# Seven products of halves in both GEMMs, on blocks of 896 tokens, in an attention and MoE kernel

## The chip, the cores and the metric

One Trainium2 chip; the kernel runs on one of its cores. The metric is the device time of one execution in microseconds, the median of several. TensorE is called PE, VectorE DVE, ScalarE ACT, GpSimd POOL and SyncE SP; almost all transfers are issued from SP's queue.

## The reference

```python
# attention, per batch b and head h (8 x 8, 576 tokens, 64 wide)
q_s = softmax(q, over the 64 columns)
k_s = softmax(k, over the 576 tokens)
kv  = k_s.T @ v                    # 64 x 64
out = q_s @ kv                     # 576 x 64
x = all heads side by side         # 4608 tokens x 512
# MoE
h = x @ w_in                       # 512 -> 2048
g = h * clip(h + 3, 0, 6) / 6
y = g @ w_out                      # 2048 -> 512, float32
```

The weights come as float64. Each float32 operand of the two GEMMs is held as a sum of two parts, hi + lo (type fp32r), and a product is made in three matmuls: hi·hi, hi·lo and lo·hi.

## The kernel before

The 4608 tokens go in nine blocks of 512 (`TB`). w_in and w_out are cut into sixteen pieces `f` of 128 columns (rows) of the hidden width; a pair is two neighbouring pieces.

**Blocks 0 and 1** are plain. For each f, `gemm1` (12 matmuls of 512 columns into the PSUM tile `ph`) makes 128 hidden features for 512 tokens; ACT (L560) and DVE (L561) make the gate g; `split` (L121: ACT casts the hi part at L123, an engine, mostly DVE, subtracts at L124) makes g_hi and g_lo; `gemm2` (12 matmuls of 512 columns) adds g times w_out into four accumulators `po`, tokens on partitions. During block 0, `load_w` and `decode` bring in the sixteen weight pieces and turn them into hi and lo parts; DVE does most of that. During block 1, `fast_weights` (L454 to L465) makes for each pair of w_in, on DVE, the four sums of quarters that seven-product multiplication (Strassen's method in Winograd's form) needs, splits them, and stores seven pieces of 256 KB per pair in DRAM (`wf`).

**Blocks 2 to 8** run pair by pair in `fast_pair`. GEMM1 of a pair is seven products; each is six matmuls of 256 columns (half of the 512 tokens), with its weight piece fetched back from DRAM into a ring of twelve (`fetch`, `RING`). Three PSUM tiles x, y, z (ring `ph`, two banks, and `pz`) gather the products; ACT and DVE (L517 to L543) add them up, gate and split. GEMM2 of the pair before stays plain: 24 matmuls of 512 columns. They are laid between the products by `fill(4)`, `fill(8)`, so that PE has work while ACT and DVE read a PSUM tile.

**Attention** for the next block runs as a generator, `attention`, advanced a step at a time from the block's loop. For a head pair `hp`: the softmax of q in a transposed layout (`q_softmax_t`, L284 to L302: five DVE passes over 512 columns and small copies `swap` on POOL), the softmax of k (L333, L348, L351), the matmuls `pkv`, and `px`, which is x for 128 features by 512 tokens, in hi and lo parts. `x_factors` makes from x the seven token-side operands: four differences on POOL (L437 to L440), splits on ACT and DVE.

**Order of the work.** From block 1 on, PE's matmuls keep the program's order (`keep_in_program_order`). The other engines' instructions are put in an order by a scheduler at build time, and run in that order.

Of the kernel before, what the change touches and what calls it, by code (L numbers as in the profile page):

```python
# [18 lines left out]
P = 128  # L19
TB = 512  # L20
QD = 32
NC4 = TB // P
EPS = 1e-9
# [7 lines left out]
def attention_moe(  # L31
# [8 lines left out]
    out: bass.AP,  # L40
):

# [20 lines left out]
    NT, DM = out.shape  # L63
    NB = NT // TB
    NFC = w.shape[0]
    NCC = DM // P
# [3 lines left out]
    SHIFT = S - TB  # L70

    const = ctx.enter_context(tc.tile_pool(name="const", bufs=1))
    wp = ctx.enter_context(tc.tile_pool(name="wp", bufs=1))
# [35 lines left out]


    def place(f, dt, name):
        return wp.tile([P, 4 * DM], dt, name=name, tag=f"w{f}")
# [8 lines left out]
    def split(hi, lo, src, engine=nc.vector):  # L121

        nc.scalar.copy(hi, src)  # L123
        engine.tensor_sub(lo, src, hi.bitcast(F32))  # L124

    def load_w(f, sides=(0, 1)):
        if f not in raws:
            raws[f] = place(f, U32, f"raw{f}")
        a, b = 2 * DM * sides[0], 2 * DM * (sides[-1] + 1)
        nc.sync.dma_start(  # L130
            raws[f][:, a:b], w[f].rearrange("p s n -> p (s n)")[:, a:b]
        )

    def decode(f):

# [15 lines left out]
        v = moe.tile([P, n], F32, name="v", bufs=2)  # L151
# [15 lines left out]
    FAST = 2  # L167
    x_tiles = {}

    def x_block(j):  # L170
        if j not in x_tiles:
            x_tiles[j] = (
                xp.tile([P, NCC, TB], F32R, name=f"x_hi{j}", tag="x_hi"),
                xp.tile([P, NCC, TB], F32R, name=f"x_lo{j}", tag="x_lo"),
            )
        return x_tiles[j]
# [24 lines left out]
    def kv_of(j, hp, ke, vt):  # L201

        pkv = ps_a.tile([P, TB], F32, name="pkv", tag="pa")
# [8 lines left out]
        kv = att.tile([P, P], F32, name="kv", bufs=5)  # L212
# [10 lines left out]
    def kv_split(j, hp):  # L223
        kv = kvs[j, hp]
        kvs[j, hp] = (
            att.tile([P, P], F32R, name=f"kv_hi{j}_{hp}", tag="kv_hi", bufs=5),
            att.tile([P, P], F32R, name=f"kv_lo{j}_{hp}", tag="kv_lo", bufs=5),
        )
        split(*kvs[j, hp], kv)

# [6 lines left out]

# [22 lines left out]
    def k_softmax(j, km, ke, kt):  # L260

# [3 lines left out]
        pool, tag = (ps_a, "pa") if j else (ps_o, "po")  # L265
        pe = pool.tile([P, TB], F32, name="pe", tag=tag)
        pe2 = pool.tile([P, TB], F32, name="pe2", tag=tag)
# [6 lines left out]
    NG = TB // QD  # L274
# [5 lines left out]

# [6 lines left out]
    def q_softmax_t(qt):  # L287

# [12 lines left out]
        qT = moe.tile([P, 2 * DM], F32, name="m", bufs=1)[:, 0:TB]  # L301
# [3 lines left out]
    def attention(j, hp):  # L305

        early = j < 2  # L310
        if not j:
            kt, qt, qT, vt, ke = first[hp]
        else:
            if j < B:
                kt = att.tile([P, S], F32, name="kt", bufs=1)
                nc.sync.dma_start(kt, kT[j, hp])
                ke = att.tile([P, NCH, P], F32, name="ke", bufs=2)
                if not early:
                    nc.sync.dma_start(ke, k[j, hp].rearrange("p c h d -> p c (h d)"))
                vt = att.tile([P, NCH, 2, D + 1], F32, name="vt", bufs=2)  # L320
                nc.sync.dma_start(vt, v[j, hp])
            qt = att.tile([P, TB], F32, name="qt", bufs=2)
            nc.sync.dma_start(qt, q[j, hp] if early else qf[j - 2, hp])
            if early:
                qt = qt.rearrange("p (c h d) -> p c h d", c=NC4, h=2)

        if j < B:
            km = att.tile([P, 1], F32, name="km", bufs=2)
            if early:
                ks = k_softmax(j, km, ke, kt)  # L330
# [35 lines left out]
        if j < B:  # L366
            kv_of(j, hp, ke, vt)
            if not early:
                kv_split(j, hp)
# [382 lines left out]
```

## Time and profile before

| | |
|---|---|
| time, median of 3 runs | 916.43 us (916.09 to 917.74) |
| span of the profiled execution | 914.7 us |
| median less span | 1.7 us |
| mean granted TensorE clock | 0.989 |
| first product of block 2 starts | 248.35 us |
| matmuls | 5380 |
| moved by DMA | 182.04 MB, mean 199 GB/s |

No time of its own is listed for the profiled execution; its span is the first to the last instruction, and the 1.7 us are what lies around it. A busy time of an engine is the part of the span in which at least one of its instructions ran; instructions of one engine overlap a little, so the sum of their durations is some per cent more. A matmul's duration in the groups (394 ns for 512 columns) is from its start to its modelled end and holds the pipeline; how long it keeps PE is read from the distance of starts.

### The profile page before, as it was taken

What the parts mean: (1) busy time and instruction counts of PE and PEld (TensorE: products, weight loads), DVE (VectorE), ACT (ScalarE), POOL (GpSimd) and SP (SyncE); (2) the same over time, 40 slices, a digit from 0 to 9 for tenths busy, and PEclk for the clock granted to TensorE, in tenths of its full rate; (3) what the DMA queues carried; (4) which work ended last, traced back from release to release, by engine and by line L of the source; (5) the groups of instructions that cost most, each with busy time, mean ns of one, the idle gap of its engine ahead of it and who ended that gap; (6) DMA issues with size and microseconds to landing.
All of it is one profiled execution on the core that took longest, in us unless ns stands there. A gap on an engine that the chain in (4) does not pass through costs nothing.

```text
span 914.7 us, 15285 instructions
## 1 busy us (share of the span) xinstructions
PE 863.9 (94%) x5380; PEld 740.6 (81%) x5380; DVE 629.0 (69%) x1265; ACT 456.1 (50%) x938; POOL 147.2 (16%) x330
## 2 busy tenths in 40 slices
PE   4799998999989999999999999999989999999998
PEld 3478766778878888888878888888878898999887
DVE  7999997888876666766666666767666655444333
ACT  6897653444444444445444444445544444444333
POOL 4112232121312120212011211112121201010000
PEclk8899999999999999999999999999999999999999
DMA  9973242538666667666676667765755565557641
GB/s 373 415 311 98 85 151 100 161 117 299 190 221 193 213 197 255 204 212 200 223 225 196 213 210 252 212 208 176 237 162 166 169 207 170 176 165 228 183 140 46
DMA packets 96842, 182.04 MB, mean 199 GB/s; under 512 B 9728, under 2 KB 24064, under 8 KB 94720
## 3 DMA queue, kind: packets, MB, share of 16 engines
q1 hardware_dynamic: 96192, 180.03, 60.9%
q10 hardware_dynamic: 576, 1.05, 0.3%
q8 instruction: 43, 0.70, 0.3%
q14 instruction: 31, 0.25, 0.1%
HBM read 156.93 MB, written 24.12 MB: 198 GB/s over the span
## 4 chain that ended last, share of the span: by engine, by line
PE 66%; DVE 10%; DMA 5%; ACT 2%; issue 1%; POOL 1%; SPq 0%; DVEq 0%; ACTq 0%; POOLq 0%
PE po L91 32%; PE ph L91 25%; PE pz L91 4%; DMA out_dram<-ob 3%; DMA qt<-in_qf_dram 2%; PE px L91 2%; PE pkv L91 2%; DVE m L302 1%; DVE x_lo L124 1%; DVE qT_lo L124 1%; DVE x_hi L124 1%; POOL swap L284 1%; ACT qT_hi L123 1%; DVE ob L591 1%; ACT v L433 1%
## 5 line engine op out<-in xcount | busy, mean ns | idle before, releaser
L91 PE MATMUL po<-w,w 128*128 128x512 f32 x1008 | 261.5, 394 | 2.2 <-DVE ob L591 2.2
L91 PEld LDWEIGHTS po<-w,w 128*128 128x128 f32 x1008 | 178.4, 189 | 32.8 <-DVE ob L591 4.0
L91 PE MATMUL ph<-w,w 128*128 128x256 f32 x1008 | 140.1, 284 | 16.7 <-DVE second L526 16.3
L91 PE MATMUL ph<-x_lo,w 128*128 128x256 f32 (+1 forms) x800 | 151.5, 304 | 2.1 <-ACT second L522 1.1
L91 PEld LDWEIGHTS ph<-w,w 128*128 128x128 f32 x1008 | 132.1, 190 | 24.2 <-DVE second L526 18.7
L91 PE MATMUL ph<-x_hi,w 128*128 128x256 f32 (+1 forms) x592 | 137.7, 337 | 3.1 <-DVE w L124 1.8
L91 PEld LDWEIGHTS ph<-x_lo,w 128*128 128x128 f32 x800 | 116.9, 189 | 16.2 <-ACT second L522 1.4
L91 PEld LDWEIGHTS ph<-x_hi,w 128*128 128x128 f32 x592 | 92.9, 191 | 16.7 <-DVE w L124 3.2
L123 ACT CAST w<-g 128x512 fp32r<-128x512 f32 x112 | 69.5, 620 | 73.7 <-DVE g L535 39.3
L124 DVE TENSOR_TENSOR w<-g,w 128x512 fp32r<-128x512 f32 x112 | 77.7, 694 | 27.5 <-ACT w L123 26.6
L91 PE MATMUL po<-w 128*128 128x512 f32 x336 | 86.2, 393 | 0.0
L124 DVE TENSOR_TENSOR qT_lo<-m,qT_hi 128x512 fp32r<-128x512 f32 x28 | 23.5, 839 | 80.8 <-ACT qT_hi L123 80.8
L91 PE MATMUL po<-w,g_hi 128*128 128x512 f32 x256 | 69.5, 409 | 2.2 <-ACT g_hi L123 2.0
L91 PEld LDWEIGHTS po<-w 128*128 128x128 f32 x336 | 59.6, 189 | 10.4 <-ACT w L123 0.5
L533 ACT ACTIVATE g<-ph,three 128x256 f32<-128x256 f32 x56 | 26.5, 472 | 72.2 <-PE ph L91 72.2
L284 POOL COPY swap<-qm 32x16 f32<-32x16 f32 x112 | 35.8, 319 | 159.2 <-DVE qm L292 133.4
L91 PEld LDWEIGHTS po<-w,g_hi 128*128 128x128 f32 x256 | 47.4, 191 | 14.4 <-ACT g_hi L123 4.0
L535 DVE SCALAR_TENSOR_TENSOR g<-g,ph 128x256 f32<-128x256 f32 x56 | 23.3, 415 | 45.2 <-ACT g L533 44.9
L526 DVE TENSOR_TENSOR second<-second,ph 128x256 f32<-128x256 f32 x56 | 22.8, 406 | 43.8 <-ACT second L525 43.7
L91 PE MATMUL pz<-x_hi,w 128*128 128x256 f32 x336 | 51.5, 290 | 0.0
L91 PEld LDWEIGHTS pz<-x_hi,w 128*128 128x128 f32 x336 | 46.5, 190 | 4.4
L525 ACT COPY second<-ph 128x256 f32<-128x256 f32 x56 | 20.9, 373 | 55.4 <-PE ph L91 55.3
(123 smaller groups left out, 1290.5 us busy)
## 6 DMA issues: line engine op xcount, KB each, us to landing
w<-wf SPq DMA_DIRECT2D x392, 256.0 KB, 2.9
raw<-in_w_dram SPq DMA_DIRECT2D x16, 1024.0 KB, 12.9
out_dram<-ob SPq DMA_DIRECT2D x36, 256.0 KB, 2.8
vt<-in_v_dram SPq DMA_DIRECT2D x28, 325.0 KB, 3.7
wf<-w SPq DMA_DIRECT2D x16, 512.0 KB, 4.6
kt<-in_kT_dram SPq DMA_DIRECT2D x28, 288.0 KB, 3.1
ke<-in_k_dram SPq DMA_DIRECT2D x24, 320.0 KB, 3.1
qt<-in_qf_dram SPq DMA_DIRECT2D x28, 256.0 KB, 3.0
```

Source lines behind the costliest of these rows:

```text
L91: nc.tensor.matmul(out, lhsT, rhs, start=start, stop=stop, skip_group_check=goes_on)
L123: nc.scalar.copy(hi, src)
L124: engine.tensor_sub(lo, src, hi.bitcast(F32))
L284: nc.gpsimd.tensor_copy(swap[r : r + QD], stat[o : o + QD])
L302: nc.vector.transpose(qT, qt)
L433: nc.scalar.copy(x[:, TB:], px)
L525: nc.scalar.copy(second[:, HT:], x)
L526: nc.vector.tensor_add(second[:, HT:], second[:, HT:], y)
L533: nc.scalar.activation(a, h, AF.Relu, bias=three, scale=1.0)
L535: nc.vector.scalar_tensor_tensor(a, a, 6.0, h, op0=ALU.min, op1=ALU.mult)
L591: nc.vector.tensor_scalar_mul(ob, po[t], 1.0 / 6.0)
```

## The change

- **Blocks.** Blocks 0 and 1 stay plain. The other 3584 tokens go in four large blocks of 896 (`SB`), halves of 448 (`TH`).
- **Phase 1** (`phase1`): GEMM1 of all eight pairs, 56 products of six matmuls of 448 columns; the seven products of neighbouring pairs are interleaved by a table (`AT`). PSUM tiles x1, y1, z1 come from a pool of six banks. g of the whole block stays on chip as float32 (`g_pairs`), not split.
- **Phase 2** (`phase2`): GEMM2 by the same seven products, again 56 of six matmuls of 448 columns, grouped by product (`ORDER2`, eight pairs each), with the output features on partitions. For each product `make` splits a quarter of g (or a running sum of quarters, L589, L591, L593) into a ring of four (`gf`), three products ahead of PE. The output is written transposed, and the host side of `kernel` turns it back.
- **Weights.** Both w_in and w_out are now kept as seven pieces per pair. `sum_weights` makes the sums: ACT copies the hi part of four quarters (L430), four DMAs issued from POOL add the lo part in flight (`accum_op=ALU.add`, L431), DVE makes four sums, `split` follows. Thirteen of the sixteen calls are in block 1, three (`late_sums`) in the first phase 1. The plain quarters are stored by `plain_weights`.
- **Attention** of a large block (`sb_attention`): q's softmax over 896 columns, one or two new batches of k and v per head pair, and `px` as float32 matmuls without hi and lo parts; x stays float32, and `factors` makes the seven operands on ACT and DVE, none on POOL.
- **Memory.** The weights lie in two pools that are closed in turn (`next_stage`): the operands and the ring of fetched pieces (five tiles of two pieces) take the place of w_0 to w_9, the tiles g0 to g6 that of w_10 to w_15.

The core of the diff:

```diff
+TH = 448
+SB = 2 * TH
...
-    ps_h = ctx.enter_context(tc.tile_pool(name="ps_h", bufs=2, space=PSUM))
-    ps_o = ctx.enter_context(tc.tile_pool(name="ps_o", bufs=4, space=PSUM))
+    ps = ctx.enter_context(tc.tile_pool(name="ps", bufs=6, space=PSUM))
...
+    def sb_attention(s, hp):
+        t0 = START + s * SB
+        need = [b for b in range(t0 // S, (t0 + SB - 1) // S + 1)]
...
+        qT = q_softmax_t(qt)
+        yield
...
+        for c in range(2):
+            px = bank_a("px")
...
+                    mm(px[:, lo:hi], kvs[b, hp], qT[:, sl], True, True)
+            nc.scalar.copy(x[:, hp, c * TH : (c + 1) * TH], px[:, 0:TH])
...
+    AT = {1: 0, 0: 1, 3: 3, 2: 4, 4: 6, 5: 9, 6: 12}
+    SLOTS1 = sorted((7 * p + AT[n], p, n) for p in range(NPAIR) for n in range(7))
+    SLOTS1 = [(p, n) for _, p, n in SLOTS1]
+    ORDER2 = (1, 2, 3, 0, 4, 6, 5)
+    SLOTS2 = [(p, n) for n in ORDER2 for p in range(NPAIR)]
...
+    def sum_weights(pair, side):
+
+        w4 = moe.tile([P, 2 * DM], F32, name="v", bufs=3)
...
+            for n, src in enumerate(halves(pair, side)):
+                t = w4[:, n * HT : (n + 1) * HT]
+                nc.scalar.copy(t, src[:, 0].bitcast(F32))
+                nc.gpsimd.dma_start(t, src[:, 1].bitcast(F32), accum_op=ALU.add)
...
+        nc.vector.tensor_add(s1, a21, a22)
+        nc.vector.tensor_sub(s2, s1, a11)
+        nc.vector.tensor_sub(s3, a11, a21)
+        nc.vector.tensor_sub(s4, a12, s2)
+        for i in range(2):
...
+            split(four[:, :, 0], four[:, :, 1], src)
+            for k_ in range(2):
+                block = (S1, S2, S3, S4)[2 * i + k_]
+                keep(pair, side, block, dst[:, k_ * TB : (k_ + 1) * TB].bitcast(F32))
...
+    def factors(s):
...
+        parts(X11, x11)
+        yield
+        parts(X21, x21)
+        yield
+        t = moe.tile([P, 2, TB], F32, name="r", tag="gp", bufs=3)[:, :, 0:TH]
+        nc.vector.tensor_sub(t, x22, x12)
+        parts(T3, t)
...
+    def phase1(s, between):
...
+            for c in range(2):
+                cs = slice(c * P, (c + 1) * P)
+                for m, (w_, f_) in enumerate(((w_hi, f_hi), (w_hi, f_lo), (w_lo, f_hi))):
+                    mm(to, w_[:, cs], f_[:, c], n in (0, 1, 2) and not c and not m, c == 1 and m == 2, True)
+            used(s, 0, i)
...
+                if n == 1:
+                    nc.scalar.copy(h11, x)
+                if n == 0:
+                    nc.vector.tensor_add(h11, h11, z)
+                    relu6(h11, temp()[:, 0, 0:TH], h11)
+                if n == 3:
+                    nc.scalar.copy(h21, x)
+                if n == 2:
+                    nc.scalar.copy(h22, y)
+                if n == 4:
+                    nc.vector.tensor_add(h22, h22, x)
+                if n == 5:
+                    relu6(h12, temp()[:, 0, 0:TH], x)
+                if n == 6:
+                    nc.vector.tensor_add(h21, h21, y)
+                    r = temp().rearrange("p a n -> p (a n)")[:, 0:SB]
+                    relu6(gb, r, gb)
+                    nc.vector.tensor_sub(h12, h22, h12)
...
+    def phase2(s, between):
...
+        def make():
...
+            t = ring[:, i % 4]
+            split(t[:, 0], t[:, 1], src)
+            ready[i] = t
+            if n == 1:
+                nc.vector.tensor_add(a, a, b)
+            if n == 2:
+                nc.vector.tensor_sub(b, d, a)
+            if n == 0:
+                nc.vector.tensor_sub(c, c, a)
...
-    for j in range(FAST, NB):
-        for pair in range(NFC // 2):
...
-            gs = fast_pair(j, pair, slot)
-            fill()
-            pend.append(work(j, [2 * pair, 2 * pair + 1], gs))
+    for s in range(NS):
...
+        def between1(i):
+            if not s and i in (12, 24, 36):
+                sum_weights(*late_sums[i // 12 - 1])
+            if i % 5 in (1, 3):
+                next(step, None)
+
+        def between2(i):
+            if i > 16 and i % 2:
+                next(step, None)
+            if i in (31, 33, 35, 37, 39, 41, 43):
+                next(fac, None)
+
+        phase1(s, between1)
+        phase2(s, between2)
```

Two places show how the instructions stand. On PE, before, in the middle of a fast block (`ph` and `pz` take products, `po` is GEMM2, `pm` and `pkv` attention; the names behind the arrow are the moving and the standing operand):

```order
L91 MATMUL ph<-x_hi_311,w_737 128x256 x6
L91 MATMUL po<-w_737,w_980 128x512 x4
L91 MATMUL ph<-w_335,w_737 128x256 x6
L91 MATMUL ph<-w_306,w_798 128x256 x6
L91 MATMUL po<-w_737,w_980 128x512 x8
L97 MATMUL pm<-ident,kb 128x128
L91 MATMUL ph<-x_lo_312,w_798 128x256 x6
L91 MATMUL po<-w_798,w_1039 128x512 x8
```

On PE now, the first products of a phase 1 (x, y, z are its PSUM tiles, `right` the token-side operands, `left` the fetched weight pieces):

```order
L87 MATMUL x_2537<-right_2444,left 128x448 x6
L87 MATMUL z_2546<-right_2447,left 128x448 x6
L87 MATMUL x_2537<-right_2492,left 128x448 x6
L87 MATMUL y_2601<-right_2452,left 128x448 x6
L87 MATMUL x_2537<-right_2495,left 128x448 x6
L87 MATMUL x_2622<-right_2444,left 128x448 x6
L87 MATMUL z_2633<-right_2447,left 128x448 x6
```

The four or eight matmuls of GEMM2 that stood between two products are gone; between two products into the same tile x stand products of the other tiles and of the neighbouring pair.

On DVE, before, about one pair of a fast block (`first`, `second` and `ph` belong to the products, `w` takes the split g, `x_hi`, `x_lo` the split operands, `kv`, `qT_lo` and `m` are attention):

```order
L519 TENSOR_TENSOR first<-first,pz 128x256
L124 TENSOR_TENSOR kv_lo_2_3732<-kv,kv_hi_2_3731 128x128
L535 SCALAR_TENSOR_TENSOR g<-g,first 128x256
L124 TENSOR_TENSOR qT_lo<-m,qT_hi 128x512
L124 TENSOR_TENSOR x_hi_311<-v,x_hi_311 128x256
L124 TENSOR_TENSOR x_lo_312<-v,x_lo_312 128x256
L302 STREAM_TRANSPOSE m<-qt 128x512
L526 TENSOR_TENSOR second<-second,ph 128x256
```

On DVE now, in the fourth group of products of the first phase 2 (`gf` is the ring of split quarters of g, `g` a tile of g, `right` and `x_1535` belong to the operands of the next block):

```order
L593 TENSOR_TENSOR g_2544<-g_2544 128x448
L124 TENSOR_TENSOR right_3792<-r,right_3792 128x896
L124 TENSOR_TENSOR gf<-g_2855,gf 128x448
L593 TENSOR_TENSOR g_2631<-g_2631 128x448
L647 TENSOR_TENSOR v<-v 128x448 x2
L509 TENSOR_TENSOR x_1535<-x_1535 128x2x448
L124 TENSOR_TENSOR gf<-g_2963,gf 128x448
L124 TENSOR_TENSOR right_3839<-x_1535,right_3839 128x896
L124 TENSOR_TENSOR gf<-g_3075,gf 128x448
```

Between two splits of g, one for each product of PE, now stand a subtraction of 448 columns and one or two operations of 896 columns.

More of the change, by code (lines that the diff above doesn't have):

```diff
@@ L201, in kv_of @@
     def kv_of(j, hp, ke, vt):
[L203 removed]
+        pkv = bank_a("pkv")
         for c in range(NCH):
@@ new lines, in attention_moe, with x_of @@
+    held = {}
+    def x_of(s):
+        if "x" not in held:
+            held["x"] = xp.tile([P, NCC, SB], F32, name="x32", tag="xa")
+        return held["x"]
+    def sb_attention(s, hp):
+        t0 = START + s * SB
+        need = [b for b in range(t0 // S, (t0 + SB - 1) // S + 1)]
+        qt = att.tile([P, SB], F32, name="qt", bufs=2)
+        nc.sync.dma_start(qt, qf[s, hp])
+        loads = {b: load_k(b, hp, tokens=True) for b in need if (b, hp) not in kvs}
+        new = {}
+        for b, (kt, ke, vt) in loads.items():
+            km = att.tile([P, 1], F32, name="km", bufs=2)
+            nc.vector.tensor_reduce(km, kt, axis=AX.X, op=ALU.max)
+            kb = att.tile([P, P], F32, name="kb", bufs=2)
+            nc.gpsimd.tensor_copy(kb, km.broadcast_to([P, P]))
+            new[b] = ke, vt, kb
+        qT = q_softmax_t(qt)
@@ new lines, in attention_moe, with keep, halves @@
+    SLOT = [{pn: i for i, pn in enumerate(slots)} for slots in (SLOTS1, SLOTS2)]
+    NSLOT = len(SLOTS1)
+    late_sums = [(7, 0), (6, 1), (7, 1)]
+    kept = [dr.tile([P, NSLOT, TB], F32, name=f"wf{i}") for i in range(2)]
+    spare = dr.tile([P, len(late_sums), TB], F32, name="spare")
+    def keep(pair, side, block, src):
+        to = kept[side][:, SLOT[side][pair, PRODUCT[block]]]
+        nc.sync.dma_start(to, src)
+    def halves(pair, side):
+        a, b = (wi, wo)[side][2 * pair], (wi, wo)[side][2 * pair + 1]
+        one, two = a[:, :, 0:HT], a[:, :, HT:]
+        if side:
+            return one, b[:, :, 0:HT], b[:, :, HT:], two
+        return one, two, b[:, :, HT:], b[:, :, 0:HT]
@@ new lines, in attention_moe, with work @@
+    accs = {}
+    done2 = []
+    def work(j, n, f, g):
+        if j not in accs:
+            accs[j] = [bank("po") for _ in range(NTT)]
+        gemm2(f, *g, accs[j], n == 0, n == NFC - 1)
+        if n == NFC - 1:
+            store(j, accs[j])
+        if j and f % 2:
+            plain_weights(f // 2, 1)
+            if (f // 2, 1) not in late_sums:
+                sum_weights(f // 2, 1)
+        if j and f == EARLY - 1:
+            next_stage(0)
+            fetch(GROUPS)
+    LAG = 2
@@ new lines, in attention_moe @@
+    fac = factors(0)
+    for f in range(NFC):
+        g = gemm1(1, f)
+        if f % 2:
+            plain_weights(f // 2, 0)
+            if (f // 2, 0) not in late_sums:
+                sum_weights(f // 2, 0)
+        for _ in range(1 if f % 4 == 1 else 2):
+            next(step, None)
+        for args in pend:
+            work(*args)
+        pend = [(1, f, f, g)]
+        if f >= 14:
+            for _ in range(3):
+                next(fac, None)
+    for args in pend:
+        work(*args)
```

597 lines of the change are left out of this document (300 added, 297 removed).

## The prediction

> **What bounds the kernel now.** First the page's busy times, then the same by stretch of the span: blocks 0, 1, 2, 3 and most of the last one.
>
> ```profile
> span 914.7 us, 15285 instructions
> PE 863.9 (94%) x5380; PEld 740.6 (81%) x5380; DVE 629.0 (69%) x1265; ACT 456.1 (50%) x938; POOL 147.2 (16%) x330
> ```
> ```profile
> core 0: us, PE busy (x) PEld busy (x) DVE busy (x) ACT busy (x) POOL busy (x), PEclk, DMA share, GB/s
> 0.00:146.50 146.50, 123.82 (x640) 93.50 (x640) 138.97 (x206) 104.32 (x197) 40.47 (x49) 0.95 0.62 229
> 146.50:250.00 103.50, 100.14 (x515) 79.84 (x515) 87.47 (x187) 47.39 (x88) 21.62 (x51) 0.98 0.55 178
> 250.00:348.00 98.00, 92.18 (x625) 81.56 (x624) 67.53 (x151) 47.01 (x101) 16.26 (x49) 0.98 0.67 209
> 348.00:444.00 96.00, 92.17 (x635) 81.45 (x634) 65.09 (x144) 46.02 (x100) 15.64 (x44) 1.00 0.68 215
> 800.00:905.00 105.00, 105.00 (x658) 94.48 (x656) 42.52 (x86) 40.33 (x87) 2.50 (x3) 1.00 0.51 157
> ```
>
> The 94% is a mean over stages with different limits. In block 0 DVE is busy 139.0 of 146.5 us: decoding is the limit. From block 1 on it is PE, idle 3.4 us there and 3.8 in block 3, where DVE has 31 us to spare. In the last block, without attention, PE never stops. The chain of waits, and two instants of the timeline, give what a matmul costs:
>
> ```profile
> 854.83 1.44 PE ph L91 x12
> 856.26 1.84 PE po L91 x8
> ...
> 875.93 1.44 PE ph L91 x12
> ...
> 905.27 5.79 PE po L91 x24
> ...
> 911.08 0.69 DVE ob L591
> ```
> ```profile
> 227.07 0.39 PE L91 MATMUL px<-qT_hi,kv_hi 128*128 128x384 f32 x1
> 227.31 0.34 PE L91 MATMUL px<-qT_lo,kv_hi 128*128 128x384 f32 x1
> 227.48 0.34 PE L91 MATMUL px<-qT_hi,kv_lo 128*128 128x384 f32 x1
> 227.66 2.02 PE L91 MATMUL po<-w,g_hi 128*128 128x512 f32 x8
> ...
> 248.35 0.87 PE L91 MATMUL pz<-x_hi,w 128*128 128x256 f32 x6
> ```
>
> Twelve of 256 columns in 1.435 us are 119.6 ns each, eight of 512 in 1.84 are 230. A line through both is 9.2 ns + 0.4313 ns a column: 448 columns take 202.4 ns. The rows of 384 columns, starting 175 ns apart, lie on it (174.8). Check: a pair is 42 x 119.6 + 24 x 230 = 10.54 us, and the two pairs from 854.83 to 875.93 took 21.10.
>
> **PE's work, part by part.** Products before: seven blocks of eight pairs, 7 x 8 x 10.54 = 590.3 us. Now: four blocks of 112 products of six matmuls, 2688 x 202.4 ns = 544.0 us. The gain is 46.3 us: 37 from columns (1,290,240 to 1,204,224 at 0.4313 ns), 9 from starts (3696 to 2688 at 9.2). A product keeps PE 1.214 us, eight of them 9.7.
>
> The Trainium skill ("TensorE: Matmul & The Clock Gate", Back-to-back issue gap) gives a warm gap of N/2.4 + 2.5 ns: 189 ns for 448 columns, 508 us for the products, and a sum 36 us lower than mine. The trace disagrees, with 230 ns at 512 where the page has 216; the measured line decides.
>
> Attention on PE, from the timeline:
>
> ```profile
> 116.07 0.91 PE L91 MATMUL px<-qT,kv 128*128 128x448 f32 x2
> 116.82 0.60 PE L97 MATMUL pe<-ident,kt 128*128 128x128 f32 x4
> ...
> 195.65 0.27 PE L97 MATMUL pm<-ident,kb 128*128 128x128 f32 x1
> ...
> 201.44 0.95 PE L91 MATMUL pkv<-vt,ke 128*64 128x65 f32 x20
> 202.32 2.12 PE L91 MATMUL po<-w,g_hi 128*128 128x512 f32 x8
> ```
>
> px in float32, 448 columns: 0.75 us, so 1.5 per head pair and large block. pkv 0.88, pm about 0.1 (estimate, between 0.03 and 0.27). The blocks are prepared one ahead and need 2, 1, 2, 1 new batches: 4 x (1.5 + 1.96) = 13.8 us, or 4 x 2.48 = 9.9. The first 13.8 falls into block 1 (before: 4 x (0.88 + 0.1 + 3 x 0.23) = 6.7), the rest, 9.9 + 13.8 + 9.9 = 33.6, among the products.
>
> **DVE's work.** PE gets less to do per token, DVE more, so the question is where DVE's list outgrows PE's. Prices:
>
> ```profile
> L540 DVE TENSOR_TENSOR second<-second,ph 128x256 f32<-128x256 f32 x56 | 23.0, 411 | 0.0
> L294 DVE TENSOR_TENSOR qt<-qt,qm 128x512 f32<-128x512 f32 x28 | 19.2, 684 | 0.4
> L333 DVE TENSOR_REDUCE km<-kt 128x1 f32<-128x576 f32 x24 | 17.8, 743 | 0.0
> L348 DVE TENSOR_TENSOR ke<-ke,pm 128x640 f32<-128x640 f32 x24 | 19.6, 816 | 5.9 <-PE pm L97 5.9
> L213 DVE SCALAR_TENSOR_TENSOR kv<-pkv,rk,mask 128x128 f32<-128x128 f32 x32 | 11.0, 345 | 0.7
> ```
>
> The line through 256 and 512 columns gives 0.616 us for 448 and 1.09 for 896. I priced every DVE instruction in both lists so. For block 3 the sum is 69.7 against 65.1 busy: instructions overlap a little, factor 0.94.
>
> *Block 0* gains 4.9 us of list (154.9 against 150.0: the first softmaxes are wider), 4.5 on the span, since DVE is the limit there.
>
> *Block 1*: thirteen sums of 4 x 0.411 + 2 x 0.684 = 3.0 are 39.1 us (before: eight of 4.4); four softmaxes over 896 columns with two batches each, some of it already in block 0; eleven operations of `factors`, 12.0. The list is 118.1 against 98.6. The 98.6 took 87.5 busy, so 105 to 110 now. PE needs 100.1 + 7.1 = 107.2, and 110.6 with its idle 3.4. Two nearly full engines that wait for each other: 115 us (111 if PE alone sets it, 124 if the list runs at its full sum with 6 of waits), 11.5 more. DVE's end counts: tile g0 takes the place of w_10, whose last sums are its last work there, and the fourth product waits for the copy into g0. The first product starts at 248.35 + 4.5 + 11.5 = 264.3.
>
> *Large blocks.* DVE's lists are 147, 147, 119 and 93 us (x 0.94: 138, 138, 111, 87) against 146, 150, 146 and 136 on PE. On the mean PE still bounds, but the work is uneven. Between the split for the first product of the n = 0 group and that of the next group stand 15 operations of 448 columns, 8 of 896 and a small one: a list of 18.2, so 17.1 us, beside 9.7 of PE. From pair 7's z to the first split of the second group the list is 19.3 and 19.8 in the first two blocks, so 18.2 and 18.6 us beside twelve products, 14.6. The ring lets DVE fall three products, 3.6 us, behind. Going through all stretches so, PE loses 8 us in each of the first two large blocks, 3 in the third, nothing in the last: 19 us. A wait in DVE's queue (for a swap from POOL, for late sums arriving by DMA) delays all gates behind it and so the release of x and y. That I price like the idle time of today's block 3, 3.8 in 96 us, so 11 over the 450 us that hold attention; its bounds are nothing and 18 (5.8 per 98, block 2).
>
> **ACT and transfers** I cost at nothing, on a group of casts and two rows of DMA issues (KB each, us to landing).
>
> ```profile
> L123 ACT CAST w<-g 128x512 fp32r<-128x512 f32 x112 | 69.5, 620 | 73.7 <-DVE g L535 39.3 <-DVE g L543 34.3
> ```
> ```profile
> w<-wf SPq DMA_DIRECT2D x392, 256.0 KB, 2.9
> out_dram<-ob SPq DMA_DIRECT2D x36, 256.0 KB, 2.8
> ```
>
> ACT is busy 46 of 96 us now; over 896 tokens that is 80, less 28 casts of g, plus 56 narrower ones, at 0.62 at most: below 98 in 150. If that cover is gone, each late cast costs PE its 0.6.
>
> A weight piece stays 256 KB; at block 3's 215 GB/s for 0.68 of the engines it needs 0.83 us against 1.21 of its product, and ten are fetched ahead. They share SP's queue with the loads of k, v and q, whose waits for a free buffer hold them up; ten products, 12 us, cover that.
>
> **Tail.** Before, 0.7 for the scaling and 2.8 for landing (span's end 3.6 after PE). Now two ACT scalings and 448 KB: 5.2, an estimate from the same rows.
>
> **Sum.** 264.3 + 544.0 + 33.6 + 19 + 11 + 5.2 = 877.1 of span; 1.7 around it (916.43 - 914.7): **879**.
>
> **Rivals.**
>
> *B, PE alone.* DVE's surplus is taken up by the lists around it: its mean share, 92%, speaks for it, the order of the instructions against. Less 19 and 4 in block 1: 856; without the 11 as well, 845.
>
> *C, DVE has no slack.* If instructions overlap less (factor 1) and the three products of lead are always used up, the stretches above PE add to 48 us rather than 19: 908; with the 124 in block 1, 917. For it: block 1 needs DVE and PE at once. Against: DVE reached 139.0 of 146.5 in block 0, with overlap.
>
> *D, slower: the sums by POOL's DMAs.* No DMA of the trace is issued by POOL. Block 1 has 52 that add to a copy that ACT has just written. If each held POOL's queue until it landed, at 2.8 us as the 256 KB rows, that is 146 us, and with the swaps and copies of four head pairs, at 0.32 and 0.34, 158 instead of 115:
>
> ```profile
> L284 POOL COPY swap<-qm 32x16 f32<-32x16 f32 x112 | 35.8, 319 | 159.2 <-DVE qm L292 133.4 <-DVE rk L211 22.3
> L335 POOL COPY kb<-km 128x128 f32<-128x128 f32 x24 | 8.2, 340 | 39.9 <-PE pm L97 37.1 <-DVE qr L298 2.1
> ```
>
> The time is then 922; it becomes slower from 2.7 us each. Against it: SP issues on without waiting for landings, and the queue shows waits of such a DMA for ACT and for one eight DMAs earlier, not for the last. The Trainium skill ("DMA: Bandwidth & Descriptors", Anatomy of one DMA) fits such a DMA with 2.0 us plus bytes over 436 GB/s, 2.3 us for these, most of it completion: even in series 132 us in block 1, and 896. No run here shows it yet.
>
> *E, the width does not pay.* If 448 columns kept PE as long as 512, 2688 x 27.6 ns = 74 us more, 953. The rows of 384 columns speak against it.
>
> **Chances.** Forecast 0.46, B 0.22, C 0.17, D 0.09, E 0.03, and 0.03 for a sum of small waits that ends where it began. C's upper end takes 0.01 to the slower side. A measurement here tells 0.2%, 1.8 us, from no change. Faster 0.84, same 0.03, slower 0.13. The range, 846 to 912, holds the forecast, B and nearly all of C; D and E, 0.12, lie outside with the 0.03.
>
> **What would show it.** Right: products with 448 columns starting 0.202 us apart; 2688 of them; the first at 264 (255 to 275); PE idle gathered around the change of phases and the n = 0 group, released by a split into `gf`; the last large block near 136 us; its PE time without gaps. Wrong: PE waiting for `left` or for ACT; a block 1 beyond 125 us with POOL's DMAs on the chain (D); gaps in all stretches of the first two large blocks (C); none (B); matmuls 0.23 apart (E).

## The result, and the profile after

The changed kernel takes 925.28 us (median of 4 executions, 923.06 to 926.50), the one before 916.26 beside it: a ratio of 1.0093, 95% interval 1.0065 to 1.0122. It is slower by 0.9%, where 879 was forecast, and lies beyond the range of 846 to 912. The profiled execution has a span of 923.5 us, 46.4 more than the forecast sum of 877.1.

First the profile page of the changed kernel: busy times, then the granted clock and the DMA share in 40 slices of the span, then the queue of DMAs that POOL issues (packets, MB, share of 16 engines' time).

```profile
span 923.5 us, 12980 instructions
PE 841.9 (91%) x4328; PEld 722.7 (78%) x4328; DVE 711.8 (77%) x1193; ACT 486.6 (53%) x858; POOL 141.0 (15%) x242
...
PEclk9889996999987798999999999999999999999999
DMA  9994545898997896875788887577756668666674
...
q0 software_dynamic: 9216, 8.39, 5.9%
```

PE has less to do, as forecast, and is idle for longer. After the first slices its clock falls to 0.6 to 0.8 in slice 7 (from 139 us, the boundary of blocks 0 and 1), in slices 12 to 14 (from 254 us, the end of block 1) and in slice 16, in the first large block. The four large blocks by stretch of the span (columns: length, busy time and count of PE, PEld, DVE, ACT, POOL, then clock, DMA share, GB/s):

```profile
289.90:468.90 179.00, 159.99 (x782) 139.52 (x780) 138.91 (x242) 84.71 (x144) 24.56 (x48) 0.93 0.79 253
468.90:628.70 159.80, 155.01 (x874) 138.47 (x873) 130.99 (x231) 82.83 (x140) 14.87 (x40) 0.99 0.77 253
628.70:780.60 151.90, 149.62 (x782) 132.41 (x781) 109.71 (x182) 78.19 (x133) 2.77 (x10) 1.00 0.69 218
780.60:919.10 138.50, 137.72 (x673) 125.83 (x671) 88.11 (x144) 65.34 (x113) 0.00 (x0) 1.00 0.66 213
```

The forecast's terms, shared out over these blocks (136 of products each; attention 9.9, 13.8, 9.9; DVE's overload 8, 8, 3; a third of the 11 for waits in each of the first three), are 157.6, 161.5, 152.6 and 136.0. Three of the four came within 2.5 us; the first is 21.4 too long. The first product, forecast at 264.3, started at 289.93, and block 1's first gate, 151.5 by the forecast (147.03 of before plus 4.5), at 158.21. So the miss of 46.4 has three places: 6.7 ahead of block 1's first gate, 18.9 in block 1 (131.7 from there to the first product, forecast 112.8), 21.4 in the first large block. All the rest together is -0.6.

PE's timeline at the first product, and its larger waits around it (in brackets the idle time and what ended it):

```profile
205.93 3.33 PE L87 MATMUL px<-m,kv 128*128 128x128 f32 x8 [5.86 <-DVE qr L305]
...
289.93 1.39 PE L87 MATMUL x<-right,left 128*128 128x448 f32 x6
...
297.13 2.61 PE L87 MATMUL x<-right,left 128*128 128x448 f32 x6 [4.59 <-ACT g L552]
...
310.88 4.85 PE L87 MATMUL x<-right,left 128*128 128x448 f32 x12 [4.49 <-DVE g L561]
...
349.48 2.61 PE L87 MATMUL x<-right,left 128*128 128x448 f32 x6 [5.99 <-DVE g L561]
```

At 205.93 PE waits for DVE, and DVE had stood still until an adding DMA landed. Its row there, and the sum of such waits of DVE between 157 and 272 us; then the group of DMAs on POOL (busy, mean ns; idle before them), and their row among the DMA issues (KB each, us to landing):

```profile
204.76 0.42 DVE L434 TENSOR_TENSOR v<-v 128x256 f32<-128x256 f32 x1 [4.77 <-DMA v<-w]
```
```profile
DVE v L434 <- DMA v<-w: 19.9, 9, 4.8
```
```profile
L431 POOL DMA_DIRECT2D v<-w x52 | 45.7, 1000 | 64.6 <-ACT v L430 28.3
...
v<-w POOLq DMA_DIRECT2D x52, 128.0 KB, 5.6
```

Five microseconds of it, seen in stretches of the span:

```profile
195.00:200.00 5.00, 5.00 (x22) 3.76 (x21) 4.99 (x12) 2.64 (x6) 2.07 (x4) 1.00 1.09 269
200.00:205.00 5.00, 0.07 (x1) 0.00 (x0) 0.24 (x1) 1.20 (x4) 2.12 (x5) 0.93 1.05 345
205.00:210.00 5.00, 4.07 (x11) 3.34 (x12) 5.00 (x13) 2.72 (x5) 1.73 (x2) 0.50 0.75 129
```

From 200 to 205 PE and DVE do almost nothing while the DMA engines are all busy (share 1.05); after that pause PE runs at half its clock. The eight px matmuls at 205.93 took 3.33 us. The Trainium skill ("TensorE: Matmul & The Clock Gate", What's actually happening) has the clock halve after an idle window of about 3.4 us; the trace agrees, with 0.50 after 5.86 us.

In the first large block the tie is less direct. At 297.13 PE waits for ACT, whose queue held casts of block 1's sums and the last output of block 1. At 310.88 it waits for DVE, which had waited for a copy on POOL; that copy stood in POOL's queue behind the adding DMAs of a late sum, and the first of these had waited 14.9 us for a load:

```profile
303.74 2.69 POOL L426 DMA_DIRECT2D v<-wf  x3 [14.94 <-DMA v<-wf]
...
309.55 0.75 DVE L341 TENSOR_REDUCE km<-kt 128x1 f32<-128x576 f32 x1 [6.50 <-POOL kb L343]
```

### The profile page after: what moved, and what is told of

It is laid out like the page before. It is cut to its first block, busy times and chain, and to the rows that moved or that the text cites. A ratio compares the mean times of both kernels' runs of the same rounds, so it can differ in the third digit from the quotient of the medians.

```text
span 923.5 us, 12980 instructions
## 1 busy us (share of the span) xinstructions
PE 841.9 (91%) x4328; PEld 722.7 (78%) x4328; DVE 711.8 (77%) x1193; ACT 486.6 (53%) x858; POOL 141.0 (15%) x242
## 3 DMA queue, kind: packets, MB, share of 16 engines
q0 software_dynamic: 9216, 8.39, 5.9%
q10 hardware_dynamic: 576, 1.05, 0.3%
## 4 chain that ended last, share of the span: by engine, by line
PE 52%; DVE 23%; issue 9%; DMA 9%; POOL 4%; ACT 2%; SPq 0%; DVEq 0%; ACTq 0%; POOLq 0%
PE x L87 28%; PE y L87 11%; PE z L87 9%; DMA v<-w 3%; POOL v L431 2%; PE px L87 2%; DVE gf L124 2%; DVE v L144 2%; DMA kt<-in_kT_dram 2%; DVE right L124 2%; DVE v L148 2%; DVE g L522 2%; DVE w L124 1%; DMA v<-spare 1%; DVE gp L124 1%
## 5 line engine op out<-in xcount | busy, mean ns | idle before, releaser
L87 PE MATMUL x<-right,left 128*128 128x448 f32 x768 | 178.4, 380 | 16.3 <-DVE g L561 11.7
L123 ACT CAST gf<-g 128x448 fp32r<-128x448 f32 x224 | 126.7, 567 | 125.7 <-PE x L87 57.0
L87 PEld LDWEIGHTS x<-right,left 128*128 128x128 f32 x768 | 146.7, 193 | 33.4 <-DVE g L561 13.0
L87 PE MATMUL x<-gf,left 128*128 128x448 f32 x768 | 163.9, 369 | 4.8 <-DVE gf L124 4.5
L124 DVE TENSOR_TENSOR gf<-g,gf 128x448 fp32r<-128x448 f32 x224 | 135.8, 618 | 38.6 <-ACT gf L123 37.1
L87 PEld LDWEIGHTS x<-gf,left 128*128 128x128 f32 x768 | 144.5, 189 | 20.9 <-DVE gf L124 9.1
L87 PE MATMUL po<-w,gp 128*128 128x512 f32 x384 | 104.4, 422 | 6.4 <-DVE gp L124 3.6
L87 PE MATMUL ph<-x,w 128*128 128x512 f32 x384 | 100.0, 408 | 2.3 <-DVE x L124 1.5
L87 PE MATMUL z<-gf,left 128*128 128x448 f32 x384 | 83.2, 372 | 5.8 <-DVE gf L124 5.5
L87 PE MATMUL y<-right,left 128*128 128x448 f32 x384 | 87.5, 374 | 0.0
L431 POOL DMA_DIRECT2D v<-w x52 | 45.7, 1000 | 64.6 <-ACT v L430 28.3
```

The costliest lines, as they stand in the source:

```text
L87: nc.tensor.matmul(out, lhsT, rhs, start=start, stop=stop, skip_group_check=goes_on)
L431: nc.gpsimd.dma_start(t, src[:, 1].bitcast(F32), accum_op=ALU.add)
```

## The experiments

Theory T at the start: the adding DMAs of the weight sums are what lengthens block 1 and the first large block. R1: DVE's list and PE bound these stretches together, whatever the sums do. R2: the DMA engines are full there. All times are medians; ratios are to the kernel before, run on the same chip.

| | time, us | ratio (95% interval) | first product | large block 1 | 2 |
|---|---|---|---|---|---|
| changed kernel | 925.28 | 1.0093 (1.0065 to 1.0122) | 289.9 | 179.0 | 159.8 |
| e1_no_adds | 887.83 | 0.9694 (0.9666 to 0.9722) | 272.6 | 160.3 | 159.6 |
| e2_pool_adds | 902.55 | 0.9842 (0.9815 to 0.9869) | 282.7 | 157.2 | 161.5 |
| e3_pool_early | 904.07 | 0.9868 (0.9853 to 0.9883) | 283.4 | 163.8 | 160.0 |
| e4_dve_adds | 904.54 | 0.9869 (0.9848 to 0.9890) | 277.9 | 171.1 | 160.1 |
| e5_plain_dma | 900.60 | 0.9829 (0.9808 to 0.9851) | 276.4 | 165.7 | 162.0 |
| e6_lag | 922.53 | 1.0073 (1.0048 to 1.0098) | 283.5 | 181.3 | 160.3 |
| e10_two_dma | 924.81 | 1.0081 (1.0055 to 1.0107) | 283.4 | 178.5 | 159.1 |
| e7_kt2 | 918.59 | 1.0024 (1.0007 to 1.0041) | 278.2 | 183.1 | 159.8 |
| e13_adds_aside | 915.76 | 0.9994 (0.9969 to 1.0019) | 297.4 | 159.0 | 159.6 |
| e15_swaps_act | 929.62 | 1.0156 (1.0131 to 1.0181) | 292.1 | 181.2 | 159.5 |
| e16_plain_aside | 916.23 | 1.0011 (0.9994 to 1.0029) | 299.1 | 160.3 | 160.8 |
| e11_wide_dve | 895.63 | 0.9780 (0.9737 to 0.9824) | 280.3 | 158.0 | 160.0 |
| e12_wide_dve_kt2 | 883.50 | 0.9646 (0.9612 to 0.9680) | 268.9 | 159.7 | 159.8 |
| e14_no_diffs | 871.90 | 0.9514 (0.9480 to 0.9549) | 268.9 | 155.2 | 157.5 |

The stage times are each kernel's profiled execution. Of e2, e10 and e13 that one was 5, 7 and 3 us below the median, so their first products may read early by that much.

**Without the adding DMAs** (e1_no_adds).

```diff
                 nc.sync.dma_start(t, src[:, 0:HT])
-                nc.gpsimd.dma_start(t, src[:, HT:], accum_op=ALU.add)
...
                 nc.scalar.copy(t, src[:, 0].bitcast(F32))
-                nc.gpsimd.dma_start(t, src[:, 1].bitcast(F32), accum_op=ALU.add)
```

> The 64 DMAs that add a lo part to a copy of its hi part are left out, in the thirteen early sums and the three late ones; the sums are then those of the hi parts alone (that part of the work is left out), everything else stays: the copies by ACT, the sums and splits on DVE, the stores and loads. Theory T, the adding DMAs' time to landing lengthens the sums' chain (copy, DMA, sums, split, store) and PE idles for it: first fast product at 262 to 272 us instead of 289.9, the first large block 157 to 163 us instead of 179, the time 880 to 892. Rival R1, DVE's own list and PE bound these stretches together: first product at 285 or later, first large block above 174, time 917 or more. Rival R2, the DMA engines are full there (share near 1) and other transfers wait: 8 MB less of some 32 in block 1, so the first product at 280 to 285 and the time 912 to 918.

37 us are gone: 887.8. Its page, its first product, and 157 to 270 us of the span, ahead of which stands the same stretch of the changed kernel:

```profile
157.00:270.00 113.00, 102.18 (x547) 81.38 (x547) 81.81 (x168) 57.22 (x118) 51.11 (x83) 0.93 0.91 241
```
```profile
PE 826.4 (93%) x4328; PEld 709.4 (80%) x4328; DVE 710.2 (80%) x1193; ACT 485.7 (55%) x858; POOL 92.7 (10%) x178
...
PEclk9889997899999999999999999999999999999999
```
```profile
157.00:270.00 113.00, 107.48 (x592) 85.88 (x591) 103.16 (x201) 71.82 (x140) 16.51 (x40) 0.98 0.68 241
```
```profile
201.59 1.76 PE L87 MATMUL px<-m,kv 128*128 128x128 f32 x8 [0.90 <-DVE kv L200]
...
272.57 1.38 PE L87 MATMUL x<-right,left 128*128 128x448 f32 x6
```

DVE fills 103 of 113 us where it filled 82; the DMA share falls from 0.91 to 0.68. The same 4328 matmuls keep PE busy for 826.4 us instead of 841.9: these 15.5 us go with the slower clock (mean 0.954 for 0.979) that came with the waits (the eight px matmuls: 1.76 against 3.33). T holds, R1 falls. R2 expected 7 to 13 of these 37 us, because it counted bytes.

**Other ways to add.** e2_pool_adds: POOL adds; e3_pool_early: POOL adds in the early sums alone; e4_dve_adds: DVE adds.

```diff
-                nc.scalar.copy(t, src[:, 0].bitcast(F32))
-                nc.gpsimd.dma_start(t, src[:, 1].bitcast(F32), accum_op=ALU.add)
+                nc.gpsimd.tensor_add(t, src[:, 0].bitcast(F32), src[:, 1].bitcast(F32))
...
                 nc.sync.dma_start(t, src[:, 0:HT])
-                nc.gpsimd.dma_start(t, src[:, HT:], accum_op=ALU.add)
+                nc.sync.dma_start(t_lo, src[:, HT:])
+                nc.gpsimd.tensor_add(t, t, t_lo)
```

> All sixteen sums: POOL adds hi and lo itself (tensor_add over 512 columns) in place of ACT's copy and the adding DMA; the three late sums load both parts by SP into two tiles. The result is the reference's. Theory T: 52 additions at about 1.0 us (estimate, 0.7 to 1.3) keep POOL some 55 us busy and the chain is shorter by the 5.6 us of each landing: first product at 264 to 274, first large block 157 to 166, time 882 to 897. R1 (DVE and PE bound): 917 or more. R2 (DMA engines full): as in the run without the adds, 912 to 918. A loss of its own, POOL and DVE sharing a path to memory, would show as longer DVE additions in block 1 and a first product beyond 280.

> As the run with POOL's additions, but for the thirteen early sums only; the three late ones keep their adding DMAs. The result is the reference's. Theory T: the first product as in that run (264 to 274), the first large block 170 to 179 still, so the time 15 to 20 us above that run's, 898 to 912. If the late sums are not what lengthens the first large block (its losses come from DVE's list, or from what block 1 left behind), the block falls to 157 to 166 here too and the two times agree within 4 us.

> As the run with POOL's additions, but the additions on DVE: 52 x 0.68 = 35 us more on DVE in block 1 and 12 x 0.68 = 8 us in the first large block, no DMA and no copy by ACT. The result is the reference's. Theory T with DVE's list as the next limit: block 1 takes 130 to 145 us, first product at 280 to 292, first large block 160 to 170, time 900 to 918. If DVE had slack in block 1 (PE or the DMAs bound it), the first product comes at 264 to 274 and the time is 880 to 897. R1 (DVE bounds it already): first product 35 us later than after's, beyond 320, and a time above 945.

All three beat the kernel before, by 1.3 to 1.6%, and none reaches e1_no_adds. POOL's additions cost DVE: its groups from 160 to 270 us, of e1_no_adds and then of e2_pool_adds, with the mean of one behind the busy time.

```profile
L124 DVE TENSOR_TENSOR w<-v,w 128x512 fp32r<-128x512 f32 x26 | 17.6, 681 | 0.9 <-ACT w L123 0.8
...
L434 DVE TENSOR_TENSOR v<-v 128x256 f32<-128x256 f32 x13 | 5.5, 423 | 0.0
```
```profile
L124 DVE TENSOR_TENSOR w<-v,w 128x512 fp32r<-128x512 f32 x26 | 20.3, 785 | 0.0
...
L438 DVE TENSOR_TENSOR v<-v 128x256 f32<-128x256 f32 x13 | 8.6, 665 | 0.0
```

The splits take 785 ns for 681, and the four sums 24 to 57% more, the third 665 for 423. This is the loss of its own that the expectation named (which speaks of additions of 512 columns; the edit adds 256 at a time). Issuing DMAs from POOL does nothing of the kind: in the changed kernel the same two rows have 680 and 418. The Trainium skill ("SBUF — State Buffer", Who interferes with whom) says that a DVE operation with two SBUF inputs contends with a POOL instruction that reads SBUF; the rows agree.

e3_pool_early misses its expectation: the two times are 1.5 us apart, not 15 to 20. With only the early sums changed, the first large block falls from 179.0 to 163.8. So most of what it lost was left behind by block 1, whose last adding DMA started at 283.7 us. In e4_dve_adds that block is still 171.1: the late additions stand in DVE's queue and wait 8.6 us there for their loads; on POOL they wait aside (157.2). (The expectation of e4_dve_adds prices its additions at the 0.68 of 512 columns; they have 256, so 52 x 0.41 = 21 us and not 35.)

**What of the adding DMA costs.** e5_plain_dma copies instead of adding (`accum_op` left out); e6_lag puts DVE's part of each sum behind the next sum's DMAs; e10_two_dma halves their number.

```diff
+        yield
         sums = moe.tile([P, 2 * DM], F32, name="v", bufs=3)
...
+    def sum_weights(*args):
+        if args:
+            unit = sum_parts(*args)
+            next(unit)
+            begun.append(unit)
+        if len(begun) > 1 or not args:
+            for unit in begun[:1]:
+                for _ in unit:
+                    pass
+            del begun[:1]
```
```diff
-            for n, src in enumerate(halves(pair, side)):
-                t = w4[:, n * HT : (n + 1) * HT]
+            for n in range(2):
+                src = (wi, wo)[side][2 * pair + n]
+                t = w4[:, n * TB : (n + 1) * TB]
                 nc.scalar.copy(t, src[:, 0].bitcast(F32))
```

> The 64 DMAs of POOL's queue stay, with their bytes, their places and their waits, but they copy the lo part over instead of adding it (the addition is left out of the sums). Theory T1, what costs is the way through a DMA in the middle of the chain, whatever it does: median time to landing still 4.5 to 6 us in block 1, first product at 284 or later, time 917 to 926. Theory T2, what costs is the addition in the DMA engines: landing falls to 2.5 to 3.5 us, first product at 272 to 280, time 895 to 908. Without the DMAs the first product came at 272.6 and the time was 888.

> The copies and adding DMAs of a sum are issued as in the changed kernel, but DVE's four operations, the splits and the stores of that sum stand one sum later in the program (in the first large block six products later), so that some 4 to 8 us of other work of DVE lie between. The result is the reference's. If the price of the adding DMA is that DVE's queue stands still until it lands (19.9 us of DVE's waiting in block 1, 25 to 30 with the first large block): first product at 272 to 280, first large block 160 to 168, time 890 to 905. If it is the throughput of POOL's queue or of the DMA engines (their share was 0.98 there), the waiting only moves: first product at 285 or later, time 915 to 927.

> Each early sum copies and adds two pieces of 512 columns instead of four of 256: 26 adding DMAs of 256 KB in block 1 for 52 of 128 KB, the same bytes; the late sums as they are. The result is the reference's. If each DMA's own cost counts (issue on POOL 0.9 us, start and completion), a sum's chain loses two of four: landing stays near 6 us, first product at 276 to 284, time 905 to 918. If bytes count, landing doubles to 9 to 11 us and the first product stays at 287 to 292, time 922 to 928.

Copying over in the same place of the same chain gives 25 of the 37 us back, as T2 expected. The queue's row on the page of e5_plain_dma, then the same queue and the issue between 157 and 270 us, of the changed kernel and of e5_plain_dma:

```profile
q0 software_dynamic: 3072, 8.39, 2.5%
```
```profile
q0 software_dynamic: 6373, 5.81, 33.4%
...
v<-w POOLq DMA_DIRECT2D x47, 128.0 KB, 5.4
```
```profile
q0 software_dynamic: 2482, 6.80, 15.9%
...
v<-w POOLq DMA_DIRECT2D x52, 128.0 KB, 4.7
```

An adding DMA is 9216 / 64 = 144 packets, a copy of the same bytes 48. The 6373 packets are those of 44.3 DMAs, so one takes 0.334 x 16 x 113 / 44.3 = 13.6 us of engine time; a copy, with 2482 packets for 51.7, takes 0.159 x 16 x 113 / 51.7 = 5.6. That is 2.4 times as much. The landing fell less than T2 expected, from 5.4 to 4.7, but DVE's waits for these DMAs between 157 and 272 us fell from 19.9 to 3.3 us. The Trainium skill ("Collectives: The Full Stack", The bandwidth ceiling) says that the reduce of a collective reads two sources and so needs two read descriptors where a copy needs one. The ratios here are 3 in packets and 2.4 in time.

e6_lag leaves the time at 922.5 and DVE's waiting at 17.4 us after 19.9, although other work stands in between. That fits sums that come through too slowly rather than single landings that DVE meets too early. e10_two_dma leaves the time as it was, while POOL's busy time from 157 to 270 us falls from 51.1 to 34.0 us: it is neither the number of DMAs nor POOL's time to issue them. (Its landing did not double, 6.2 us for 256 KB.) Packets are not the price either. The rows between 157 and 270 us of e10_two_dma, and of the plain DMAs of e16_plain_aside below:

```profile
q0 software_dynamic: 3498, 6.38, 32.1%
...
q10 hardware_dynamic: 13534, 12.33, 33.2%
```

An adding DMA of 256 KB has 144 packets too, and half the packets take almost the same share of the engines (32.1% for 6.38 MB, 33.4% for 5.81). Those plain DMAs of 128 KB have 144 each as well, and took 6.4 us of engine time, half of an adding one.

POOL's queue is held up as well. Before 11 of the 52 adding DMAs of the changed kernel POOL stands still, 12.8 us in all, for nothing that the profile shows. Counted by the packets of q0, POOL starts none while more than two earlier ones are unfinished; with the copies of e5_plain_dma it is up to three. The 52 start 2.2 us apart, from 168.7 to 283.7. In e10_two_dma these pauses come to 0.7 us in block 1, and the time stays, so they are not the price either.

**Out of the chain, and off POOL's queue.** e13_adds_aside: e1_no_adds, and each ACT copy is also added to a place in DRAM. e15_swaps_act: the changed kernel with the softmaxes' copies on ACT. e16_plain_aside: e13's adding DMAs replaced by twice as many plain ones from ACT's queue.

```diff
                 nc.scalar.copy(t, src[:, 0].bitcast(F32))
+                nc.gpsimd.dma_start(aside[:, next(turn)], t, accum_op=ALU.add)
```
```diff
-            nc.gpsimd.tensor_copy(swap[r : r + QD], stat[o : o + QD])
+            nc.scalar.copy(swap[r : r + QD], stat[o : o + QD])
...
-                nc.gpsimd.tensor_copy(kb, km.broadcast_to([P, P]))
+                nc.scalar.copy(kb, km.broadcast_to([P, P]))
```
```diff
                 nc.scalar.copy(t, src[:, 0].bitcast(F32))
+                for _ in range(2):
+                    nc.scalar.dma_start(aside[:, next(turn)], t)
```

> As the run without the adding DMAs (first product at 272.6, 888 us), but each of the 52 copies by ACT in block 1 is also added by a DMA of POOL's queue to a place in DRAM that nobody reads: the same 128 KB each, outside of the sums' chain. The lo parts are left out of the sums, as there. Theory T3, the adding DMAs cost by the time they take of the DMA engines (33% of all sixteen's time in block 1, where the mean share was 0.83 to 0.98), so that loads and stores of others come late: first product at 279 to 290, time 895 to 912, though no sum waits for them. Theory T4, they cost by standing in the chain (copy, DMA, sums), by landing 5.6 us late: first product at 271 to 275, time 885 to 892.

> The changed kernel, adding DMAs and all, with the softmaxes' copies (swap and kb, 0.2 to 0.4 us each, 64 and 16 of them) on ACT instead of POOL, so that POOL's queue holds the adding DMAs alone in block 1. The result is the reference's. If the adding DMAs cost by holding up these copies in POOL's queue: first product at 270 to 280 instead of 289.9. If they cost by the DMA engines' time: first product at 285 or later, first large block 172 or more, and the time 918 to 930 (ACT has the room, but its queue is in order too).

> As the run with the adding DMAs aside (first product at 297.4, 915.8 us), but each is replaced by two plain DMAs of 128 KB from ACT's queue, behind the copy that they read, to a place in DRAM that nobody reads; POOL issues no DMA. The lo parts are left out of the sums. By their share of the engines' time in block 1 (plain: 57.6% of sixteen engines for 21.3 MB in the changed kernel, some 6 engine-us for 128 KB; adding: 33.4% for 5.8 MB, some 13) the two load the DMA engines alike. If the engines' time is the price: first product at 283 to 298, time 900 to 916. If POOL's queue is: first product at 271 to 277, time 886 to 894.

With no sum that needs their result, the 52 early adding DMAs still cost 28 us (915.8 against 887.8), more than T3 expected, all of it in block 1. They are not quite the same DMAs: to DRAM one takes 15.9 us of engine time (42.6% for 6963 packets between 157 and 270 us) where it took 13.6, and the share of all engines is 0.98. T4, a sum that waits for its own operand, falls. One tie is left, as the waits of DVE in e13_adds_aside show, and then the largest of ACT in e16_plain_aside:

```profile
DVE v L436 <- DMA aside<-v: 8.5, 6, 3.2
```
```profile
ACT w L123 <- DMA aside<-v: 49.5, 10, 7.7
```

The DMAs hold a buffer of `v` until they have read it, for which DVE waited 8.5 us and ACT 11.4, together as much as the 19.9 before; and 49.5 us of ACT's queue in e16_plain_aside are waits for them. e16 therefore loses the expected time, but does not tell full engines from held-up buffers. e15_swaps_act is clearer: with POOL's queue free of the softmaxes' copies the first product still comes at 292.1 and the time is 929.6. Copies that stood behind the DMAs in POOL's queue were then not the price, unless ACT's queue, which is in order too, took the gain. To take other traffic out of block 1 and leave the adding DMAs was not tried.

**A second buffer, and the version that is faster.** e7_kt2 gives kt two buffers; e11_wide_dve has DVE add hi and lo of 512 columns at a time, POOL only the late ones; e12_wide_dve_kt2 has both.

```diff
-        kt = att.tile([P, S], F32, name="kt", bufs=1)
+        kt = att.tile([P, S], F32, name="kt", bufs=2)
```
```diff
+            for n in range(2):
+                src = (wi, wo)[side][2 * pair + n]
+                t = w4[:, n * TB : (n + 1) * TB]
+                nc.vector.tensor_add(t, src[:, 0].bitcast(F32), src[:, 1].bitcast(F32))
```

> The changed kernel with two buffers for kt instead of one, nothing else. Of the 25.6 us that the first product came late, some 7 stood ahead of block 1's first gate (158.2 us against 151.5 forecast), where three loads of kt follow one another on the chain at 138, 144 and 148 us. If the single buffer puts them in series: first gate at 151 to 154, first product at 283 to 287, time 918 to 922. If what holds them is their place in SP's queue, behind stores that wait for the decoding: first gate still at 157 to 159, the time within 2 us of 925.

> The early sums' additions on DVE, two of 512 columns a sum in place of four DMAs (26 x 0.68 = 17.8 us of DVE, against 21.5 with four of 256); the late sums' additions on POOL, with both parts loaded by SP. The result is the reference's. Theory T3: with no adding DMA the engines are free, and DVE's list is next: first product at 274 to 279 (four narrow additions on DVE gave 277.9), first large block 156 to 160 (POOL's late additions gave 156.6), time 888 to 899. If DVE's wider additions cost what four narrow ones did: 897 to 903.

> As the run with wide additions on DVE, and two buffers for kt. The result is the reference's. The second buffer alone took 6.7 us from the changed kernel (925.3 to 918.6). If that gain adds to the one of the sums, since it lies at the boundary of blocks 0 and 1: 5 to 8 us below the run with one buffer, 882 to 893. If the wait that it removes is taken up by DVE's list of block 1: within 2 us of that run.

The chain of waits of the changed kernel shows loads of kt one behind another, each followed by the maximum `km` that frees the buffer; it is this that e7_kt2 loosens:

```profile
138.37 5.52 DMA kt<-in_kT_dram
143.91 0.76 DVE km L341
144.69 2.81 DMA kt<-in_kT_dram
147.53 0.76 DVE km L341
148.31 2.74 DMA kt<-in_kT_dram
```

It takes 6.7 us off (925.28 to 918.59). The first gate stays at 158.8, against the expectation, yet PE has done 7.6 us more by 160 us (busy 134.4 for 126.9): that fits another order of the work around that gate, and why the gate itself did not move is open. e12_wide_dve_kt2 takes 883.5 us, 3.5% below the kernel before and by the two ratios 4.4% below the changed one, and it computes the whole reference. The second buffer is worth 12.1 us there, more than alone and more than the 5 to 8 expected: in e7_kt2 the first product came 11.8 us earlier too, but the first large block took 4.1 longer. From 157 to 270 us of its span, and its first product:

```profile
157.00:270.00 113.00, 103.75 (x565) 82.52 (x564) 110.79 (x215) 52.55 (x83) 15.44 (x35) 0.95 0.67 235
```
```profile
268.93 1.74 PE L87 MATMUL x<-right,left 128*128 128x448 f32 x6
```

DVE is now busy 110.8 of 113 us: it bounds block 1.

**The term for DVE's overload** (e14_no_diffs: e12_wide_dve_kt2 without the four differences of x in large blocks 2 to 4).

```diff
-        nc.vector.tensor_sub(t, x22, x12)
+        if s:
+            t = x22
+        else:
+            nc.vector.tensor_sub(t, x22, x12)
```

> As the run with wide additions and two buffers for kt, but without the four differences of x (896 columns, 1.09 us each on DVE) for large blocks 2, 3 and 4; that part of the work is left out. It tests the term of 19 us for stretches in which DVE's list is longer than PE's products, 8 in each of the first two large blocks: 4.1 us of a list of 17.1 beside 9.7 on PE are gone. If that term holds: 3 to 4 us less in each of the first two blocks, 1 to 3 in the third, 7 to 11 in all. If DVE's surplus is taken up elsewhere (the case of PE alone): within 2 us of the run with the differences.

The operands of a large block are made while the one before runs, so the time should go from blocks 1 to 3. 11.6 us less: 4.5, 2.3 and 4.3 in these, a little more than the 7 to 11 expected. In the third, PE has no gap left:

```profile
581.60:729.10 147.50, 147.50 (x782) 132.94 (x782) 105.98 (x178) 78.26 (x133) 2.79 (x10) 1.00 0.74 225
```

DVE did set the pace in those stretches. PE alone (rival B) is excluded. How much of the 8 and 8 priced for the first two blocks is real, the run doesn't show: it takes away only part of DVE's surplus there.

## Why the prediction was wrong

- **PE's price of a product held.** 2688 matmuls at 202.4 ns were forecast. The last block, by the chain of waits, has 48 in 9.71 us, 202.3 each, so rival E is out:

```profile
880.27 9.71 PE z L87 x48
889.98 9.71 PE x L87 x48
```

- **The sums of the large blocks and the tail held, in part by luck.** Large blocks 2 to 4 came within 2.5 us of their sums, the tail was 4.6 for 5.2, and e14_no_diffs shows that the overload is real. But in the third block, where that run leaves PE no gap, products and attention alone took 147.5 us for 145.9 priced, and what DVE took was 4.3 where 6.7 were priced (3 and a third of 11): two errors that cancel. The 11 for waits doesn't follow from its own rate either. 3.8 in 96 us is 17.8 over 450 us, and 5.8 in 98 is 26.6; 11 and about 18 come out when each of three blocks of 150 us is given what one of 96 had.
- **Block 1's 115 us held for all that was priced in it.** Without the adding DMAs, 113.1 us lie between the first gate (159.47) and the first product (272.57), against 112.8 forecast; the time, 887.8, is 9 above the forecast. That it is so close is in part luck: the 115 was chosen between 111 and 124.
- **The step that failed** is "ACT and transfers I cost at nothing", where the cover, "A weight piece stays 256 KB", is about the pieces fetched in the large blocks. The 52 early adding DMAs have no term in the sum at all, and the 12 late ones stand only among the waits of 11. The adding DMAs took 33% of all DMA engines' time in block 1 and 37 us of the kernel's: some 17 in block 1, some 19 in the first large block, mostly as work that block 1 left behind. 15.5 us of the 37 are PE's longer busy time, at the slower clock after its waits.
- **Rival D named the right instructions and nearly the right time (922), with 0.09.** The signs that it gave came true: block 1 took 131.7 us for its 125, and POOL's issues of adding DMAs and their landings are on the chain of waits, 14% and 21% of it from 157 to 290 us. The case against D was that such a DMA does not wait for the last one; POOL's queue did wait for earlier ones. Yet this was not the price: e10_two_dma has next to none of it in block 1 and takes the same time, and half of the loss came after block 1. That the time came so near is in part luck. The Trainium skill's fit ("DMA: Bandwidth & Descriptors", Anatomy of one DMA) gave 2.3 us for one such DMA; here it was 5.6 at the median.
- **The boundary of blocks 0 and 1** was forecast 4.5 us longer and came 6.7 beyond that. The forecast followed only DVE's list there, while the chain runs through loads of kt. A second buffer took as much off the time, but the first gate stayed at 158.8, so what made it late stays open.

What stays open is how the adding DMAs hold the others up. It is not their number, their packets or POOL's pauses (e10_two_dma), nor single landings that DVE meets (e6_lag), nor a sum that waits for its operand (e13_adds_aside). Two accounts are left. They may fill the DMA engines for everyone: the share was 0.91, and the stores of the sums (`wf<-w`) landed in 4.7 us where they took 3.6 without them. Or they may be too slow themselves, at 13.6 us of engine time each, and hold the buffers of the sums. No run parts the two.

## What to carry to other kernels

A DMA that adds is not priced like a copy of its bytes, and its packets don't tell either: look at its share of the DMA engines in the stretch where it runs. Where that stretch is already tightly shared by two engines, an addition on one of them can still cost less than one "in flight": on DVE, busy 103 of 113 us without any, wide additions gave 895.6 us where the DMAs gave 925.3. And a wait of some 5 us on PE is paid again in the clock of the matmuls that follow.

## What was not expected of the hardware

- An adding DMA of 128 KB kept POOL 0.87 us, a copying one 0.54, the engines 13.6 and 5.6 us of their time. An adding DMA of 256 KB had the same 144 packets as one of 128 KB.
- POOL started no adding DMA while more than two earlier ones were unfinished.
- A copy of the same size in the same place landed only 0.7 us sooner, and yet DVE waited 3.3 us for it where it had waited 19.9.
- POOL's additions of 256 columns (0.92 us at the median in block 1) made DVE's two-input operations in that stretch 15% (the splits) and 24 to 57% (the sums) longer.
- 4328 equal matmuls kept PE busy for 841.9 us in one kernel and 826.4 in another, at mean granted clocks of 0.954 and 0.979.
